# Turning B, C and decay rows on VectorE in 32x32 blocks of 4-byte words, in place of PE transposes

## The chip, the cores and the metric

The kernel runs on one core of a Trainium2 chip. A core has TensorE (PE in the profile; PEld is its weight load), VectorE (DVE), ScalarE (ACT), GpSimd (POOL) and SyncE (SP). They run their own instruction streams and wait for each other through semaphores. Transfers between HBM and the on-chip memory SBUF are issued here by SP and ACT. Matmul results land in PSUM. The metric is device time in microseconds (us) of one execution.

## What is computed

A chunked state-space scan over 4 sequences x 8 heads x 768 steps (head dimension 32, state 16), then a two-layer feed-forward net on its output, seen as 3072 tokens x 256.

```python
for c in range(nc):                       # chunks along a sequence
    cum = np.cumsum(log_a[:, :, sl], axis=-1)
    L = np.exp(cum[:, :, :, None] - cum[:, :, None, :]) * causal
    M = np.einsum('bhin,bhjn->bhij', Cc, Bc) * L
    y[:, :, sl] = M @ xc + (Cc @ state) * exp(cum)
    state = decay_full * state + sum_j decay_from_j * outer(Bc, xc)
g = gelu_tanh(y_as_tokens @ w_in)         # w_in 256 x 2048
out = g @ w_out                           # w_out 2048 x 256
```

The kernel uses chunks of 128 steps (24 in all, six to a sequence). It needs, for each chunk, B scaled by the suffix products of the decays a, with the 8 x 16 (head, state) pairs on partitions (`bh`), C divided by the same products, also with (head, state) on partitions and split by the parity of the head (`ce`), and B with steps on partitions (`bn`).

## The kernel before

**Units.** The chunks go through in units: chunk 0, chunk 1, and then eleven pairs. For a unit PE computes the chunk scores (`f_G`, L408, into the PSUM tile `gb`), DVE masks them (`f_M`, L418), PE makes the state update (`f_D`, L429) and y (`f_Y`, L451 and L460, into `yb`), ACT copies y out as bf16 (`f_yev`, L469, into `xm`). Then come the first matmul of the net (`f_s1`, L506), the activation (`f_gelu`, L514), the second matmul (`f_s2`, L523), the copy out of PSUM (`f_oev`, L530 or L532) and the store (`f_store`, L536).

**Preparing a sequence.** `f_clip` and `f_R` (L272, L276) form decay products in rows, one partition for each (half, sequence, head). `f_RT` (L293) and `f_RT0` (L282) turn them on PE by matmuls with an identity, `f_recip` (L305) inverts them, `f_pp`/`f_pend` (L316, L321) spread the whole-chunk products. `f_mul` (L349) scales B and C of a whole sequence, with steps on partitions; `f_T` (L358) turns six 128x128 blocks of each on PE into PSUM; `f_E` (L365, recorded at the copy helper's lines L256 or L260) copies them to SBUF; `f_F` (L373) makes `ce`; `f_N` (L379) turns `bh` back to steps on partitions and `f_bn` copies that out. The first chunk has its own short path (`f_mul0`, `f_T0`, `f_ce0`, `f_bh0`).

**Loads.** `load_bc` (L154) brings B or C of a sequence in one transfer of 384 KB; `load_bc0` (L148) brings the first chunk alone in 64 KB; `load_x` (L240) brings 128 KB a chunk; `load_wi` (L248) and `load_wo` (L252) bring the weights in quarters of 512 KB. `f_wi` (L264, recorded at L258 or L260) casts a quarter of w_in to bf16 and reorders its columns as it casts, so that `f_s1` loads 128 adjacent columns; `f_wo` casts w_out as it lies.

**Order.** `run_order` places the nodes made by `add` on the engines, by due times (`prio`), given durations and the number of buffers in each pool. The engines then run in exactly that order. While PE has nothing planned, `idle` fills in matmuls on a tile of zeros (L776).

Of the kernel before, what the change touches and what calls it, by code (L numbers as in the profile page):

```python
# [91 lines left out]

@with_exitstack
def kernel(
# [9 lines left out]
):  # L104
    nc = tc.nc
# [3 lines left out]
    Q = 128  # L109
    CPB = S // Q  # L110
    R6 = CPB
    NCH = batch * CPB
    HC = CPB // 2
    HS = S // 2
    d_ff = moe_w_in.shape[1]
    d_model = moe_w_in.shape[0]
    n_tokens = batch * S
    NF = d_ff // 128
    UNITS = [[0], [1]] + [[c, c + 1] for c in range(2, NCH, 2)]
# [3 lines left out]
    ld = ctx.enter_context(tc.tile_pool(name="ld", bufs=batch))  # L123
    wfp = ctx.enter_context(tc.tile_pool(name="wfp", bufs=6))
    ldx = ctx.enter_context(tc.tile_pool(name="ldx", bufs=NU))
    xpool = ctx.enter_context(tc.tile_pool(name="xpool", bufs=6))
    work = ctx.enter_context(tc.tile_pool(name="work", bufs=2))
    msb = ctx.enter_context(tc.tile_pool(name="msb", bufs=4))
    st = ctx.enter_context(tc.tile_pool(name="st", bufs=4))
    GT_BUFS = 6  # L130
    gpool = ctx.enter_context(tc.tile_pool(name="gpool", bufs=GT_BUFS))
    opool = ctx.enter_context(tc.tile_pool(name="opool", bufs=6))
# [5 lines left out]


    a_t = const.tile([64, HS], FP32, name="a_t")  # L140
    a_half = [bass.AP(tensor=a.tensor, offset=a.offset + i * HS, ap=[[S, batch * H], [1, HS]])
              for i in range(2)]
    XF, X16 = {}, {}
    U = [dict() for _ in range(batch)]
    bc0 = const.tile([128, 2, H, N], FP32, name="bc0")

    def load_bc0(i, q):
        q.dma_start(out=bc0[:, i], in_=(B, C)[i][0, :, 0:Q, :].rearrange("h p n -> p h n"))  # L148

    def load_bc(b, i):  # L150
        d = U[b]
        if "bc" not in d:
            d["bc"] = ld.tile([128, 2, H, R6 * N], FP32, name="bc_t")
        nc.sync.dma_start(out=d["bc"][:, i],  # L154
                          in_=(B, C)[i][b].rearrange("h (p r) n -> p h (r n)", r=R6))

    nc.sync.dma_start(out=a_t[0:32], in_=a_half[0])
    nc.scalar.dma_start(out=a_t[32:64], in_=a_half[1])
    load_bc0(1, nc.sync)
    load_bc0(0, nc.scalar)  # L160

    wz = const.tile([128, 512], BF16, name="wz")
# [3 lines left out]
    nc.scalar.activation(warm, warm, AF.Gelu_apprx_tanh)  # L166
    ends = const.tile([64, Q], FP32, name="ends")
    nc.vector.memset(ends, 0.0)
    nc.vector.memset(ends[:, Q - 1:Q], 1.0)
    ac = const.tile([64, HS + 1], FP32, name="ac")  # L170
    nc.vector.memset(ac[:, HS:HS + 1], 0.0)
    pe1 = const.tile([64, HC], FP32, name="pe1")
    pe2 = const.tile([64, 2 * batch, HC], FP32, name="pe2")

    idf = const.tile([64, 64], FP32, name="idf")
    nc.gpsimd.memset(idf, 0.0)
    nc.gpsimd.affine_select(out=idf, in_=idf, pattern=[[-1, 64]], compare_op=ALU.not_equal,
                            fill=1.0, base=0, channel_multiplier=1)
    ident = const.tile([128, 128], BF16, name="ident")
    make_identity(nc, ident)  # L180
    bmask = const.tile([128, H * D], BF16, name="bmask")
    nc.gpsimd.memset(bmask, 1.0)
    bm3 = bmask.rearrange("p (h d) -> p h d", h=H)
    nc.gpsimd.affine_select(out=bm3, in_=bm3, pattern=[[-N, H], [0, D]],
                            compare_op=ALU.is_ge, fill=0.0, base=0, channel_multiplier=1)
    nc.gpsimd.affine_select(out=bm3, in_=bm3, pattern=[[N, H], [0, D]],
                            compare_op=ALU.is_ge, fill=0.0, base=N - 1, channel_multiplier=-1)
# [4 lines left out]
    sel8 = const.tile([64, H], FP32, name="sel8")  # L192
    nc.vector.tensor_reduce(out=sel8, in_=idf.rearrange("p (b h) -> p h b", h=H),
                            op=ALU.add, axis=mybir.AxisListType.X)
    selp = const.tile([64, H, N], FP32, name="selp")
    nc.vector.tensor_copy(out=selp, in_=sel8.rearrange("p (h o) -> p h o", o=1)
                          .to_broadcast([64, H, N]))
    m8 = const.tile([64, 2 * batch], FP32, name="m8")
    nc.gpsimd.memset(m8, 1.0)
    nc.gpsimd.affine_select(out=m8, in_=m8, pattern=[[-H, 2 * batch]], compare_op=ALU.is_ge,  # L200
                            fill=0.0, base=0, channel_multiplier=1)
    nc.gpsimd.affine_select(out=m8, in_=m8, pattern=[[H, 2 * batch]], compare_op=ALU.is_ge,
                            fill=0.0, base=H - 1, channel_multiplier=-1)
    par = const.tile([128, 2], FP32, name="par")
# [5 lines left out]
    r_t = const.tile([64, HS], FP32, name="r_t")  # L210

    rt = const.tile([128, R6, batch * H], FP32, name="rt")
    pt = const.tile([128, R6, batch * H], FP32, name="pt")
    q0 = const.tile([128, H], FP32, name="q0")
    bc0s = const.tile([128, 2, H, N], BF16, name="bc0s")
    ce0 = const.tile([128, 2, Q], BF16, name="ce0")
    bh0 = const.tile([128, Q], BF16, name="bh0")
    pend = const.tile([128, NCH], FP32, name="pend")
    WF = {}
    w_in_sb = const.tile([128, 2, d_ff], BF16, name="w_in_sb")  # L220
    w_out_sb = const.tile([128, NF, d_model], BF16, name="w_out_sb")
    xm = const.tile([128, 2, n_tokens], BF16, name="xm")


    gb = ps1.tile([128, 4, 512], FP32, name="gb")
    yb = ps1.tile([128, 512], FP32, name="yb")
    y4 = yb.rearrange("p (c w t) -> p c w t", c=2, w=2)
    rp0 = yb[:, 0:H]
    T6 = [gb[:, 2 * i, 0:S // 2].bitcast(BF16) for i in range(2)]
    T6_0 = [yb[:, 0:S // 2].bitcast(BF16), T6[1]]  # L230

    T0, DT, MT, RP = {}, {}, {}, {}
    state = {}
    gts, ops, hps, outs = {}, {}, {}, {}

    def load_x(u):
        b, c = divmod(UNITS[u][0], CPB)
        XF[u] = ldx.tile([128, 2, H, D], FP32, name="x_t")
        for k in range(len(UNITS[u])):
            nc.sync.dma_start(out=XF[u][:, k], in_=x[b, :, (c + k) * Q:(c + k + 1) * Q, :]  # L240
                              .rearrange("h p d -> p h d"))

    wi = moe_w_in.rearrange("(k d) f -> d k f", d=128)
    wo = moe_w_out.rearrange("(q p k) m -> q p k m", p=128, k=4)

    def load_wi(q):
        WF[("i", q)] = wfp.tile([128, 2, 512], FP32, name="wf")
        nc.sync.dma_start(out=WF[("i", q)], in_=wi[:, :, q * 512:(q + 1) * 512])  # L248

    def load_wo(q):  # L250
        WF[("o", q)] = wfp.tile([128, 4, d_model], FP32, name="wf")
        nc.sync.dma_start(out=WF[("o", q)], in_=wo[q])  # L252
# [9 lines left out]
    def f_wi(q, k0, k1, eng):  # L262
        for k in range(k0, k1):
            copy(eng, w_in_sb[:, k, q * 512:(q + 1) * 512].rearrange("d (k p) -> d k p", k=4),  # L264
                 WF[("i", q)][:, k].rearrange("d (p k) -> d k p", k=4))

    def f_wo(q, eng):
        copy(eng, w_out_sb[:, 4 * q:4 * q + 4], WF[("o", q)])


    def f_clip(i0, i1):
        nc.vector.tensor_scalar(out=ac[:, i0:i1], in0=a_t[:, i0:i1], scalar1=1e-6, scalar2=1.0,  # L272
                                op0=ALU.max, op1=ALU.min)

    def f_R(k):
        nc.vector.tensor_tensor_scan(out=r_t[:, k * Q:(k + 1) * Q][:, ::-1],  # L276
                                     data0=ac[:, k * Q + 1:(k + 1) * Q + 1][:, ::-1],
                                     data1=ends[:, ::-1], initial=1.0,
                                     op0=ALU.mult, op1=ALU.max)

    def f_RT0():
        nc.tensor.matmul(out=rp0, lhsT=r_t[0:32, 0:Q], rhs=idf[0:32, 0:H], start=True, stop=True,  # L282
                         skip_group_check=True)

    def f_RT(r0, r1):
        if r0 == 0:
            RP[1] = psh.tile([128, 512], FP32, name="hp")[:, 0:R6 * batch * H] \
                .rearrange("p (r j) -> p r j", r=R6)
        r6 = r_t.rearrange("q (p r) -> q r p", r=R6)
        for r in range(r0, r1):  # L290
            for i in range(2):
                rs = slice(32 * i, 32 * i + 32)
                nc.tensor.matmul(out=RP[1][64 * i:64 * i + 64, r], lhsT=r6[rs, r],  # L293
                                 rhs=idf[rs, rs], start=True, stop=True,
                                 tile_position=(32 * i, 64 * i), skip_group_check=True)
# [517 lines left out]
```

## Time and profile before

| | us |
|---|---|
| Median of 3 runs (124.72 to 125.45) | 125.07 |
| Span of the profiled execution, first to last instruction | 122.8 |
| PE busy in it | 114.6 (93%) |
| DVE / ACT / POOL busy | 68.3 / 74.9 / 23.0 |
| Mean of one activation (L514), 96 of them | 0.596 |
| Mean of one mask (L418, 128x1024), 23 of them | 1.217 |
| Mean of one scaling of B or C (L349, 128x768) | 0.95 |
| Mean of one w_in cast on POOL (L258, 128x512), 6 of them | 1.193 |
| Median, issue to landing: a quarter of w_in / a chunk of x / a store | 6.9 / 4.5 / 1.7 |

PE's busy time counts its pipelined matmuls and the fill on zeros, so a busy PE is not a PE at its useful peak. The row PEclk of the profile gives the clock that PE was granted, in tenths.

### The profile page before, as it was taken

How to read it: one execution, taken by the hardware profiler on the slowest of the kernel's cores; microseconds unless marked ns; L12 is line 12 of the kernel's file. 1: busy time of each engine (PE TensorE's matmuls, PEld its weight loads, DVE VectorE, ACT ScalarE, POOL GpSimd, SP SyncE). 2: the span in 40 equal slices, each digit the busy share in tenths (PEclk: the TensorE clock that was granted, in tenths of full speed). 3: DMA queues.
4: the chain of work that ended last, by engine and by line, in shares of the span. 5: the costliest groups of instructions: out<-in, count | busy, mean ns of one | idle time of the engine just before them, and what ended most of it. 6: DMA issues, size and time to landing. Idle time of an engine off the chain costs nothing.

```text
span 122.8 us, 3507 instructions
## 1 busy us (share of the span) xinstructions
PE 114.6 (93%) x1506; PEld 96.2 (78%) x1506; DVE 68.3 (56%) x116; ACT 74.9 (61%) x145; POOL 23.0 (19%) x38
## 2 busy tenths in 40 slices
PE   5899978989799999999999999999999999999970
PEld 5687747778678798787879889787878888888860
DVE  3897999968849888184979672475663000000110
ACT  4025536674676677656686777865768766786310
POOL 7206967750320160122000000000000000000000
PEclk9975699999999999999999999999999999999999
DMA  3999959989799899851101101101110111100121
GB/s 52 242 266 265 328 112 370 320 191 200 128 229 221 127 235 216 145 134 48 43 0 48 43 0 48 43 0 48 43 43 5 45 43 45 45 21 22 43 90 43
DMA packets 40591, 14.09 MB, mean 115 GB/s; under 512 B 35904, under 2 KB 39040, under 8 KB 40576
## 3 DMA queue, kind: packets, MB, share of 16 engines
q1 hardware_dynamic: 39488, 13.75, 46.4%
q8 instruction: 12, 0.20, 0.7%
q10 hardware_dynamic: 1088, 0.11, 0.7%
q14 instruction: 3, 0.02, 0.1%
HBM read 10.72 MB, written 3.15 MB: 113 GB/s over the span
## 4 chain that ended last, share of the span: by engine, by line
PE 70%; SPq 18%; DMA 5%; DVE 3%; issue 1%; DVEq 0%
PE o_ps L523 29%; PE hp L506 29%; SPq L240 7%; DMA bc_t<-in_B_dram 5%; SPq L252 5%; SPq L154 4%; PE yb L523 3%; SPq L248 3%; PE gb L408 2%; PE yb L451 2%; PE yb L460 2%; PE gb L358 2%; DVE ch L260 2%; PE gb L379 1%; DVE bc L349 1%
## 5 line engine op out<-in xcount | busy, mean ns | idle before, releaser
L514 ACT ACTIVATE gT<-hp 128x512 bf16<-128x512 f32 x96 | 53.6, 596 | 24.4 <-PE hp L506 24.2
L506 PE MATMUL hp<-xm,w_in_sb 128*128 128x256 bf16 (+1 forms) x416 | 53.7, 267 | 0.9 <-POOL w_in_sb L258 0.4
L523 PE MATMUL o_ps<-w_out_sb,gT 128*128 128x256 bf16 x352 | 47.3, 273 | 0.0
L506 PEld LDWEIGHTS <-w_in_sb 128*128 128x128 bf16 x416 | 37.6, 99 | 7.7 <-issue 2.0
L523 PEld LDWEIGHTS <-gT 128*128 128x128 bf16 x384 | 37.1, 98 | 4.8 <-issue 0.4
L418 DVE TENSOR_TENSOR m<-gb,tri 128x1024 bf16<-128x1024 f32 (+1 forms) x25 | 29.1, 1173 | 1.9 <-PE gb L408 1.8
L532 DVE COPY o_sb<-o_ps 128x256 f32<-128x256 f32 x2 | 0.8, 424 | 25.6 <-PE o_ps L523 25.6
L258 POOL CAST x<-x_t 128x512 bf16<-128x512 f32 (+1 forms) x12 | 8.5, 710 | 25.0 <-DMA x_t<-in_x_dram 20.1
L479 DVE SCALAR_TENSOR_TENSOR s_new<-s_new,pend,hp 128x64 f32<-128x64 f32 x16 | 4.5, 279 | 11.5 <-PE hp L429 11.2
L776 PE MATMUL o_ps<-wz 128*128 128x128 bf16 x77 | 8.9, 267 | 1.3 <-DVE warm L165 1.3
L530 ACT ACTIVATE o_sb<-o_ps 128x256 f32<-128x256 f32 x20 | 7.7, 385 | 3.8 <-PE o_ps L523 2.1
L486 DVE SCALAR_TENSOR_TENSOR sp_new<-s_new,pend,bmask 128x256 bf16<-128x256 f32 x20 | 10.0, 506 | 0.0
L469 ACT ACTIVATE xm<-yb 128x512 bf16<-128x512 f32 (+1 forms) x13 | 7.3, 564 | 4.3 <-PE yb L460 2.1
L258 POOL CAST w_in_sb<-wf 128x512 bf16<-128x512 f32 x6 | 7.0, 1193 | 7.0 <-DMA wf<-in_moe_w_in_dram 7.0
L776 PEld LDWEIGHTS <-wz 128*128 128x128 bf16 x77 | 6.5, 122 | 1.8 <-DVE warm L165 1.2
L460 PE MATMUL yb<-m,x 128*32 128x128 bf16 x192 | 6.3, 223 | 0.6 <-DVE m L418 0.6
L373 DVE TENSOR_SCALAR ce<-ch,par 128x768 bf16<-128x768 bf16 (+2 forms) x10 | 5.9, 634 | 0.8 <-ACT ch L256 0.8
L451 PE MATMUL yb<-ce,sp_new 128*32 128x128 bf16 x160 | 5.3, 221 | 0.0
L408 PE MATMUL gb<-ce,bh 32*128 32x256 bf16 x96 | 5.1, 278 | 0.0
L460 PEld LDWEIGHTS <-x 128*32 128x32 bf16 x192 | 3.8, 97 | 1.5 <-issue 1.5
L358 PEld LDWEIGHTS <-bc 128*128 128x128 bf16 x48 | 3.8, 110 | 1.3 <-issue 1.1
L258 POOL CAST w_out_sb<-wf 128x1024 bf16<-128x1024 f32 x4 | 4.4, 1112 | 1.5 <-DMA wf<-in_moe_w_out_dram 1.5
(72 smaller groups left out, 61.6 us busy)
## 6 DMA issues: line engine op xcount, KB each, us to landing
x_t<-in_x_dram SPq DMA_DIRECT2D x24, 128.0 KB, 4.5
out_dram<-o_sb SPq DMA_DIRECT2D x24, 128.0 KB, 1.7
wf<-in_moe_w_in_dram SPq DMA_DIRECT2D x4, 512.0 KB, 6.9
wf<-in_moe_w_out_dram SPq DMA_DIRECT2D x4, 512.0 KB, 6.0
bc_t<-in_C_dram SPq DMA_DIRECT2D x4, 384.0 KB, 4.4
bc_t<-in_B_dram SPq DMA_DIRECT2D x4, 384.0 KB, 5.4
bc<-in_B_dram ACTq DMA_DIRECT2D x1, 64.0 KB, 4.2
bc<-in_C_dram SPq DMA_DIRECT2D x1, 64.0 KB, 2.8
```

Of the source, the lines that this page charges most:

```text
L240: nc.sync.dma_start(out=XF[u][:, k], in_=x[b, :, (c + k) * Q:(c + k + 1) * Q, :] .rearrange("h p d -> p h d"))
L258: nc.gpsimd.tensor_copy(out=o, in_=i)
L408: nc.tensor.matmul(out=gb[:, g, 256 * k:256 * k + 256], lhsT=bh_of(gc)[32 * g:32 * g + 32], rhs=ce_of(gc)[32 * g:32 * g + 32], start=True, ...
L418: nc.vector.tensor_tensor(out=MT[gc][:, g0:g1], in0=gb[:, g0:g1, 256 * k:256 * k + 256] .rearrange("p g (e t) -> p g e t", e=2), in1=tri_b ...
L451: nc.tensor.matmul(out=y4[32 * j:32 * j + 32, k, w], lhsT=sp[:, 32 * h:32 * h + 32], rhs=ce_of(gc)[:, h % 2], start=first(j), stop=False, ...
L460: nc.tensor.matmul(out=y4[32 * j:32 * j + 32, k, w], lhsT=X16[u][:, k, 32 * h:32 * h + 32], rhs=m[:, h // 2, h % 2, :], start=first(j), st ...
L486: nc.vector.scalar_tensor_tensor(out=sp_new.rearrange("p (g d) -> p g d", g=4), in0=state[("s", gc)].rearrange("p (o d) -> p o d", o=1).to ...
L506: nc.tensor.matmul(out=hp[:, j * nt:(j + 1) * nt], lhsT=w_in_sb[:, kc, fi * 128:(fi + 1) * 128], rhs=xm[:, kc, t0:t0 + nt], start=(kc == 0 ...
L514: nc.scalar.activation(gts[u][:, i * per:(i + 1) * per, 0:nt], hps.pop((u, i)).rearrange("p (j t) -> p j t", j=per), AF.Gelu_apprx_tanh)
L523: nc.tensor.matmul(out=ops[gc], lhsT=gts[u][:, fi, tt * Q:(tt + 1) * Q], rhs=w_out_sb[:, fi, :], start=(fi == 0), stop=(fi == NF - 1), ski ...
L530: nc.scalar.activation(o_sb, ops.pop(gc), AF.Copy)
L776: nc.tensor.matmul(out=zb[:, 0:128], lhsT=wz[:, 0:128], rhs=wz[:, 0:128], start=True, stop=True)
```

## The change

- **Transposes.** `f_T` now runs on DVE: pairs of neighbouring steps of bf16 make 4-byte words, and a word tile is turned in 32x32 blocks, from SBUF to SBUF. The loads put four (head pairs) x 32 partitions with 4 steps each side by side, so that blocks of 32 are enough. `f_E`, the PE transposes of B and C, the PE turns of the decays and the first chunk's own path are gone. `f_N`/`f_bn` stay on PE and ACT.
- **Decays.** Each sequence has its own `f_clip`, `f_scan`, `f_rT` (a DVE turn), `f_qT` (reciprocals, in groups of chunks) and `f_pend` (four small DVE instructions).
- **Groups.** The first sequence is prepared in groups of 1, 1, 2 and 2 chunks, the others in two groups of 3. `f_mul` is two instructions for each group, since it interleaves the steps.
- **`f_F`** masks with a bitwise AND on 4-byte integers.
- **Loads.** B and C of the first sequence come in 24 transfers of 32 KB (4 issued by ACT, 20 by SP), those of the others in 8 transfers of 96 KB each. x of the later sequences comes in one transfer of 768 KB for each sequence.
- **w_in** is cast as it lies, half of quarters 0 to 2 by ACT, the rest by POOL; `f_s1` picks every fourth column as it loads weights.
- **Units.** Chunks 0 to 3 are units of one, then pairs. `gT` has 5 buffers (6 before).
- **Last chunk.** Its second matmul is done in two halves of 128 columns, each copied out (DVE, ACT) and stored by itself.
- **Order.** A table `PRIO` gives each node a due time of its own.

```diff
+PRIO = {
+    'SP0': -401.905, "load_bc0(0, 1, 1, 'ACT')": 389.204, "load_bc0(1, 0, 1, 'ACT')": 586.494,
...
+    UNITS = [[0], [1], [2], [3]] + [[c, c + 1] for c in range(4, NCH, 2)]
...
+    def load_bc(b, i, g, q):
+        t = get("bc", b, [128, 2, 2 * CPB * R, N], FP32)
+        src = (B, C)[i]
+        QS[q].dma_start(out=t[32 * g:32 * g + 32, i].rearrange("p (k r) n -> p k (r n)", r=R),
+                    in_=bass.AP(tensor=src.tensor, offset=src.offset + (b * H + 2 * g) * S * N,
+                                ap=[[R * N, 32], [Q * N, 2 * CPB], [1, R * N]]))
+
+    def load_bc0(c, i, e, q):
...
+        QS[q].dma_start(out=t[:, i, k:k + R].rearrange("p r n -> p (r n)"),
+                    in_=bass.AP(tensor=src.tensor, offset=src.offset + e * S * N + c * Q * N,
+                                ap=[[2 * S * N, 4], [R * N, 32], [1, R * N]]))
...
+    def load_xs(b):
+        t = get("xs", b, [128, H * CPB, D], FP32)
+        nc.sync.dma_start(out=t, in_=bass.AP(tensor=x.tensor, offset=x.offset + b * H * S * D,
+                                             ap=[[D, Q], [Q * D, H * CPB], [1, D]]))
...
+    w_in5 = w_in_sb.rearrange("d k (q p j) -> d k q j p", q=4, j=4)
...
-            copy(eng, w_in_sb[:, k, q * 512:(q + 1) * 512].rearrange("d (k p) -> d k p", k=4),
-                 WF[("i", q)][:, k].rearrange("d (p k) -> d k p", k=4))
+    def f_wi(q, k, eng):
+        copy(eng, w_in_sb[:, k, q * 512:(q + 1) * 512], T[("wf", ("i", q))][:, k])
...
+    def f_rT(i):
+        nc.vector.transpose(out=rT[i].rearrange("p k r -> p r k"),
+                            in_=rr[i].rearrange("q (p r) -> q r p", r=R))
+
+    def f_qT(b, c0, c1):
+        o, v = (t[b][:, K0[b]:K0[b] + 2 * CPB] for t in (qT, rT))
+        if c1 - c0 < CPB:
+            o, v = (t.rearrange("p (e c) r -> p e (c r)", e=2)[:, :, R * c0:R * c1] for t in (o, v))
+        nc.vector.reciprocal(o, v)
...
+        for k in range(2):
+            nc.vector.tensor_tensor(
+                out=t[:, ss, :, :, k].rearrange("p s e n -> p e s n"), in0=v[:, :, ss, k],
+                in1=w[:, :, ss, k:k + 1].to_broadcast([128, 2, 2 * (c1 - c0), N]), op=ALU.mult)
+
+    def f_T(b, i, c0, c1):
+        t = get(("bT", "cT")[i], b, [128, S], BF16)
+        nc.vector.transpose(
+            out=t[:, c0 * Q:c1 * Q].bitcast(FP32).rearrange("q (c p s) -> q c s p", p=32, s=2),
+            in_=T[("bc16", (b, i))][:, 2 * c0:2 * c1].rearrange("p s e n k -> p (s e n k)").bitcast(FP32)
+            .rearrange("p (c s j) -> p c s j", s=2, j=32))
+
+    def f_F(b, c0, c1):
...
+            nc.vector.tensor_scalar(out=t[:, e, c0 * Q:c1 * Q].bitcast(I32),
+                                    in0=T[("cT", b)][:, c0 * Q:c1 * Q].bitcast(I32),
+                                    scalar1=pari[:, e:e + 1], scalar2=None, op0=ALU.bitwise_and)
...
-                                 lhsT=w_in_sb[:, kc, fi * 128:(fi + 1) * 128],
+                                 lhsT=w_in5[:, kc, fi // 4, fi % 4],
...
+    def f_s2h(h):
+        u, tt = UNIT_OF[NCH - 1]
+        o = gb[:, 2 * h, 0:128]
+        for f in range(NF):
+            nc.tensor.matmul(out=o, lhsT=T[("gT", u)][:, f, tt * Q:tt * Q + Q],
+                             rhs=w_out_sb[:, f, 128 * h:128 * h + 128], start=(f == 0),
+                             stop=(f == NF - 1), skip_group_check=True)
...
+    GROUPS = [[(0, 1), (1, 2), (2, 4), (4, 6)]] + [[(0, 3), (3, 6)]] * (batch - 1)
...
+    for n in nodes:
+        n.prio = PRIO.get(n.name, n.prio)
```

More of the change, by code (lines that the diff above doesn't have):

```diff
@@ L165 @@
     nc.vector.memset(warm, 0.0)
[L166 to L178, printed above, removed]
+    nc.vector.memset(zeros, 0.0)
+    for i in range(batch):
+        nc.vector.memset(rr[i][:, Q - 1:Q], 1.0)
     ident = const.tile([128, 128], BF16, name="ident")
     make_identity(nc, ident)
[L181 to L187, printed above, removed]
     tri = const.tile([128, Q], BF16, name="tri")
@@ L273, in f_clip, with f_warm, f_scan @@
+    def f_warm():
+        nc.scalar.activation(warm, warm, AF.Gelu_apprx_tanh)
+    def f_clip(i):
+        nc.vector.tensor_scalar(out=ac[i], in0=at[i], scalar1=1e-6, scalar2=1.0,
                                 op0=ALU.max, op1=ALU.min)
[L275 to L278, printed above, removed]
+    def f_scan(i):
+        nc.vector.tensor_tensor_scan(out=rr[i][:, 0:Q - 1][:, ::-1], data0=ac[i][:, 1:Q][:, ::-1],
+                                     data1=zeros[:, 0:Q - 1], initial=1.0,
@@ L355, in f_T @@
-    def f_T(b, i):
-        bc = U[b]["bc16"].rearrange("p i r h n -> p i r (h n)")
-        for r in range(R6):
-            nc.tensor.transpose(out=(T6 if b else T6_0)[i][:, r * 128:(r + 1) * 128], in_=bc[:, i, r], identity=ident)
-    def f_E(b, i, eng, p0=0, p1=128):
-        d = U[b]
-        nm = ("bh", "ch")[i]
-        if nm not in d:
-            d[nm] = work.tile([128, S], BF16, name=nm)
-        copy(eng, d[nm].rearrange("q (p r) -> q p r", r=R6)[:, p0:p1],
-             (T6 if b else T6_0)[i].rearrange("q (r p) -> q p r", r=R6)[:, p0:p1])
@@ new lines, in f_N, with f_bn @@
+    def f_N(b, c0, c1, where):
+        t = (gb[:, 1] if where == "gram" else psh.tile([128, 512], FP32, name="hp"))
+        T[("N", b, c0)] = t = t[:, 0:S // 2].bitcast(BF16)
+        for c in range(c0, c1):
+            nc.tensor.transpose(out=t[:, c * Q:(c + 1) * Q],
+                                in_=T[("bT", b)][:, c * Q:(c + 1) * Q], identity=ident)
+    def f_bn(b, c0, c1, eng):
+        t = get("bn", b, [128, CPB, 128], BF16)
+        copy(eng, t[:, c0:c1].rearrange("p c n -> p (c n)"), T[("N", b, c0)][:, c0 * Q:c1 * Q])
@@ L624, with load_bc0_n @@
-    mul_b = add("DVE", 0.97, f_mul, 0, 0, deps=[bl[(0, 0)], RTa, mul_c], prio=-20)
-    rtc = add("ACT", 0.33, f_rtc, deps=[RTa, mul_b], prio=-60)
-    RTa.takes("hp", rtc)
-    rc2 = add("DVE", 1.35, f_recip, 1, batch, deps=[rtc], prio=45)
-    RT0.prio = -99
-    ppn = add("PE", 0.4, f_pp, deps=[pen], prio=-28)
-    pendn = add("ACT", 0.2, f_pend, deps=[ppn], prio=-29)
-    ppn.takes("hp", pendn)
+                win_l[q] = load(1.58, load_wi, q)
+    b0l = {}
+    def load_bc0_n(*cs, act=True):
+        for c in cs:
+            for i in (0, 1):
+                b0l[(c, i)] = [load(0.16, load_bc0, c, i, e, q="ACT" if act and e else "SP", iss=0.45)
+                               for e in (0, 1)]
@@ new lines @@
+    load_bc0_n(0)
+    wrm = add("ACT", 1.3, f_warm, prio=-150)
+    xl[0] = load(0.87, load_x, 0)
+    load_w_n(0)
+    load_bc0_n(1)
+    load_w_n(1)
+    xl[1] = load(0.87, load_x, 1)
+    load_w_n(2, 3)
+    load_bc0_n(2, act=False)
+    xl[2] = load(0.87, load_x, 2)
+    load_bc0_n(3, act=False)
+    load_w_n(0, o=True)
+    xl[3] = load(0.87, load_x, 3)
+    load_w_n(1, 2, 3, o=True)
+    load_bc0_n(4, 5, act=False)
+    xl[4] = load(0.87, load_x, 4)
+    xl[5] = load(0.87, load_x, 5)
+    for b in range(1, batch):
+        an[b] = load(0.2, load_a, b)
+        load_bc_n(b, 0)
+        load_bc_n(b, 1)
+        n = load(5.2, load_xs, b)
+        for c in range(CPB):
+            xl[CPB * b + c] = n
@@ new lines @@
+    for q in range(4):
+        es = (("POOL", 0.6), ("ACT", 0.67)) if q < 3 else (("POOL", 0.6), ("POOL", 0.6))
+        win[q] = [add(e, t, f_wi, q, k, e, deps=[win_l[q]], prio=-60 + q) for k, (e, t) in enumerate(es)]
+        won[q] = add("POOL", 1.1, f_wo, q, "POOL", deps=[won_l[q]], prio=20 + q)
+        win_l[q].issue.takes("wf", *win[q])
+        won_l[q].issue.takes("wf", won[q])
+    rn, pen = {}, {}
+    for b in range(batch):
+        p0 = -100 if b == 0 else 10.0 * CPB * b - 31
+        cl = add("DVE", 0.25, f_clip, b, deps=[an[b]], prio=p0)
+        sc = add("DVE", 0.43, f_scan, b, deps=[cl], prio=p0 + 0.1)
+        rn[b] = add("DVE", 0.41, f_rT, b, deps=[sc], prio=p0 + 0.2)
+        pen[b] = add("DVE", 0.55, f_pend, b, deps=[sc], prio=-74 if b == 0 else p0 + 0.3)
@@ L673, with bnp @@
+    def bnp(b, c0, c1, deps, q, where):
+        nn = add("PE", 0.1 + 0.06 * (c1 - c0), f_N, b, c0, c1, where, deps=deps, prio=q)
+        bb = add("ACT", 0.18 + 0.08 * (c1 - c0), f_bn, b, c0, c1, "ACT", deps=[nn], prio=-65 if b == 0 else -45)
+        nn.takes(where, bb)
+        for c in range(c0, c1):
+            bnn[CPB * b + c] = bb
     for u, cs in enumerate(UNITS):
@@ L778, in idle @@
         return fill
-    pools = {"hp": 2, "o": 1, "gram": 1, "yb": 1, "wf": 6, "ob": 6}
-    for t, fn in run_order(nodes, pools, idle=idle, wait=("DVE", "POOL")):
+    pools = {"hp": 2, "o": 1, "gram": 1, "yb": 1, "wf": BUFS["wf"], "ob": BUFS["ob"]}
+    order = run_order(nodes, pools, idle=idle, wait=("DVE", "POOL"))
+    for t, fn in order:
         fn()
```

515 lines of the change are left out of this document (192 added, 323 removed), and 128 rows, old and new, of the table PRIO.

## The prediction

> **What bounds the kernel now.** I read the slices first, then the chain of waits, then PE's windows, then the timeline of the start. In the slices of the whole span (about 3.1 us each), PE is full from the tenth on; the granted clock and the load on the DMA engines say what the first third looks like:
>
> ```profile
> span 122.8 us, 3507 instructions
> PE   5899978989799999999999999999999999999970
> PEclk9975699999999999999999999999999999999999
> DMA  3999959989799899851101101101110111100121
> ```
>
> The clock is low from about 6 to 15 us, and DMA is near full, but for one slice, until 50 us. The chain that ended last, in order of time, has this around 30 us, and from 31.7 on almost nothing but PE:
>
> ```profile
> 24.08 5.77 DMA bc_t<-in_B_dram
> 29.87 0.96 DVE bc L349
> 30.82 0.88 DVE ch L260
> 31.74 0.49 PE gb L358 x6
> ...
> 34.32 0.87 PE hp L506 x8
> ...
> 66.57 0.33 PE gb L358 x6
> ...
> 119.10 0.42 DVE o_sb L532
> ```
>
> So 256 columns of the net cost 0.87/8 = 0.109 us, a transpose 0.33/6 = 0.055. Before 31.7 the end is set by transfers and the casts behind them. The windows of L506 alone (busy us and count of PE, of PEld, clock, DMA share, GB/s) show how little of the net is done early: by 24 us, 64 matmuls of half width.
>
> ```profile
> 0.00:24.00 24.00, 6.01 (x64) 4.25 (x64) 0.86 0.91 246
> 24.00:32.00 8.00, 3.88 (x28) 2.65 (x28) 1.00 1.01 186
> 32.00:119.10 87.10, 43.81 (x324) 30.69 (x324) 1.00 0.33 75
> ```
>
> The timeline of the start tells why:
>
> ```profile
> 10.04 2.13 POOL L258 CAST w_in_sb<-wf 128x512 bf16<-128x512 f32 x2 [5.85 <-DMA wf<-in_moe_w_in_dram]
> 12.51 2.21 DVE L373 TENSOR_SCALAR ce<-ch,par 128x384 bf16<-128x384 bf16 x2
> 17.02 2.06 DVE L260 CAST w_in_sb<-wf 128x512 bf16<-128x512 f32 x2
> 18.65 0.10 PEld L506 LDWEIGHTS <-w_in_sb 128*128 128x128 bf16 x1 [0.57 <-POOL w_in_sb L258]
> 20.86 3.17 SPq L154 DMA_DIRECT2D bc_t<-in_C_dram  x1
> ```
>
> The last quarter of w_in is cast at 19.1; the second sequence's C is issued from 20.9 and its B lands at 29.8.
>
> **A ledger for PE.** Counted at warm prices (0.109 us a net matmul of 256 columns, 0.055 a transpose, 0.33/8 a score matmul, 0.113/8 a matmul of y), all useful PE work of before is 98.5 us; 90.2 of it is left at 24.0, and PE ends at 119.0: it loses 4.8 us after 24. Of the work left, 36 transposes (three sequences x 2 x 6) are removed by the change.
>
> **The change, part by part.**
>
> *Transposes out of PE's stream.* 36 x 0.0547 = 2.0 us of a stream that sets the end: -2.0. The first sequence's twelve and the decay turns lie in the start, priced below.
>
> *DVE in their place.* Removed for each later sequence: two scalings at 0.955, two copies at 0.955, two `ce` at 0.475, 4.8 us. Added: eight half scalings of 192 words at 0.36 (between 0.291 for 128 and 0.955 for 768), 2.9; two reciprocals of 48 at 0.457, 0.9; `f_clip`, `f_scan`, `f_pend` at 0.19 + 0.41 + 4 x 0.17, 1.3; four masks of `f_F`, 0.25 to 0.36 each, 1.2; and the block turns, which the trace does not show. Bounds for a turn of 192 words: from the scaling row, a word a step, 0.36; from the slowest per-element DVE row but the reciprocal, the scan (0.413 for 128), 0.62. I take 0.36, since a turn is a copy without a recurrence: four make 1.4, with the decay turn 1.7. Sum 8.0, +3.2 a sequence. With masks, states and state products (6 x 1.217 + 5 x 0.27 + 5 x 0.506 = 11.2) DVE has 19.2 us for each 23.7 us of PE: hidden in the stream, by 4.5 us.
>
> *The start.* From the built order and rows of before: an issue of a small load costs SP 0.41 to 0.47, a small load lands 2.0 to 2.8 after issue, and in the built order each load waits for the one eight loads earlier to land. In before the halves of megabytes land every 1.7 to 2.6 us (9.99, 12.39, then with 128 KB between 14.46 and 17.09). Now the first quarter of w_in is SP's second issue (1.2) instead of its fifth (4.55), and only 64 KB + 4 x 32 KB go beside it: landing about 5. The second is SP's tenth; ahead of it x of chunk 0 waits for the first quarter, so issue about 6, landing 9.3. The third is the eighteenth and waits for the second: issue 9.6, landing 13. The fourth is the twenty-fifth, behind six small loads one of which waits for w_out's first quarter: issue 13, landing 16. A cast as it lies costs POOL 1.112/2 = 0.56 (the w_out row, twice the width) instead of 1.193, so the last is done near 17.2 instead of 19.1. On PE: y of chunk 0 needs two small B loads issued by ACT after its table load (3.2, landed 5.5) and then scaling, turn, mask; DVE's chain (four dependent `f_pend` steps at 0.27 apart, reciprocals at 0.2 to 0.26 among them) gives scores at 8.5 and y at 10.4, copied out behind ACT's cast of quarter two at about 11: no earlier than the 10.45 of before. From there six groups of s1 (2.6 us) are free to run before the last quarter instead of PE waiting on casts. Following PE's order: s1 of unit 1's last quarter near 17.7, y of chunk 2 at 18.2 (mask 17.8), w_out's quarters cast at 19.6, 21.1 and 23.4. By 24.0 this is 12 groups of s1 (5.2), four of s2 (1.7), six chunks of scores, five units' transposes and y: 9.0 us of work that both kernels do, where before has 6.3. So -2.7.
>
> *Its discount.* DVE has about 20 us of instructions between 3.4 and 27 in this plan, and rows of before show it slowed there: two `ce` of 384 columns took 2.21 us beside POOL's casts, when 768 take 0.475 later. If two of the new masks meet that, DVE is 1 to 1.7 us late, and y of chunks 2 to 5 with it. I add +1.0 (ends 0 and +2.3).
>
> *The second sequence.* PE's 0.62 us idle before 31.74 goes away if B and C come by then: after the last x of the first sequence (about 25) 768 KB at the 1.35 and 1.65 that its two halves took land near 28.5, scaled and turned by 30.5, when PE wants them: -0.6 (bounds 0, -0.9). x of that sequence is now one transfer behind them; six chunks at the 0.5 to 0.9 between x landings make 34, and its first cast (0.735) ends at 35, where PE's order wants it near 35: +0.7 (bounds 0, +1.5). Everything on SP queues behind it, the first stores too, but six output buffers cover those.
>
> *The end.* Two halves of 16 x 0.055 instead of 16 x 0.109, and a copy of 128 columns (0.28, as the 128x128 row of ACT) instead of 0.42: -0.1. What follows the copy, 0.33 + 1.4 to landing and 1.5 to the end, stays.
>
> Small loads are where a rule of the Trainium skill speaks against the change: "DMA: Bandwidth & Descriptors", section "Rules for kernel authors", says that transfers under 64 KB pay mostly overhead and should be joined. By it the 24 loads of 32 KB would cost little less than 24 of 64 KB; what that gives is the second rival. The rule for the strided weight load is in "SBUF — State Buffer", "Door 1": it puts the free stride at 8 bf16 or 4 fp32 elements, of which the new load uses 4. By that the third rival has no price, and the old cast's penalty (1.193 against 0.56, a stride of four fp32) is more than the page would give it, so I keep the rival.
>
> *Sum* against the profiled execution: 122.8 - 2.0 - 2.7 + 1.0 - 0.6 + 0.7 - 0.1 = 119.1 of span. The median shown is 2.3 above the span (125.07 against 122.8): 121.4.
>
> **The rivals.**
>
> *DVE too slow in the start and in each hand-over (0.14).* For: the 2.21 us row, and DVE at eight to nine tenths in slices 11 to 18 already. Against: 4.5 us of slack a sequence by the rows. With turns at the scan's price, 4 x 0.26 = 1.0 more a sequence, and masks at 1.1 beside POOL, the discount becomes its upper end and the wait for x 1.5: 121.4 + 1.3 + 0.8 + 0.4 = 123.9.
>
> *Small loads hold up the weights (0.14).* For: 25 issues on SP ahead of w_in's last quarter (eleven in before, with bigger loads). If each of the last 17 waits as long as loads of before took in a backlog (5.5 us for eight), it is issued at 4.4 + 17 x 0.69 = 16.1, lands at 21.6, is cast at 22.8, 3.7 after before. Then the start's -2.7 is lost and 3.7 is added less 1.3 for the six groups done meanwhile: 125.4, both sides of no change. Against: those landings were of 128 to 512 KB.
>
> *The strided weight load (0.10, the slower side).* `f_s1` now picks every fourth column. The trace has no strided bf16 weight load; POOL's strided cast cost twice the plain one. Weight loads of 128 adjacent columns keep pace with matmuls of 128 columns (0.055). Doubled to 0.11, the 256-column matmuls barely notice (320 x 0.003 = 1.0), but units 0 to 3 have 128 of 128 columns: +7.2, half of it inside the start's waits at best. 126.0 to 129.6; I put 128. It decides once a load passes 0.055 + 3.7/128 = 0.084 us. Below nothing there is no bound: no load gets faster.
>
> *The gain is given back (0.06).* Only the removed transposes count, and an order by 400 single due times leaves PE waiting elsewhere: about 124.8.
>
> **How the numbers follow.** Forecast 0.56 at 121.4; by its own terms 118.0 (no discount, clock not lowered at 6 to 15) to 124.2. A difference under 0.5% (124.45 to 125.70) counts as none, about what a measurement here can tell. Faster: 0.56 + 0.11 of the DVE rival + 0.02 = 0.69. Same: 0.03 + 0.05 + 0.02 = 0.10. Slower: 0.10 + 0.07 + 0.04 = 0.21. The range reaches to the middle of the strided rival: 118.0 to 127.0, leaving out about 0.08 below and 0.10 above.
>
> **What would show it.** No 128x128 transposes of B and C in PE's rows, and 24 left for `bn`. The last cast of w_in near 17 (right) or past 20 (small loads). Weight loads of w_in still at 99 ns mean, and eight half-width matmuls in 0.45 us (else the strided rival). In the chain, no DMA piece of 5 us at 24 to 30, PE from some 28 us on. Turns of 192 words at 0.36 or 0.62. PE's end at 115.4 instead of 119.0. I am wrong if PE waits on DVE's scalings or masks in the stream, or if PE's ledger at 24 us is under 8 us.

## The result, and the profile after

| | before | after |
|---|---|---|
| Median (4 runs each) | 124.89 us (124.51 to 125.45) | 134.3 us (133.22 to 134.6) |
| Span of the profiled execution | 122.8 | 132.3 |
| PE busy | 114.6 | 113.0 |

The ratio is 1.072, 95% interval [1.066, 1.078]: 9.4 us slower, where 3.7 faster was forecast and 127.0 was the top of the range. Some executions come out over 1.5% longer than the fastest of their kernel; ratios and intervals here leave them out, medians do not. In the slices of after (3.3 us each), PE has two holes, not one:

```profile
span 132.3 us, 3556 instructions
...
PE   6406994299899997786799999999999999999990
...
PEclk9955589657999999999999999999999999999999
DMA  1547665996999678999941111011001110011121
```

One hole is the start, with the DMA engines mostly at four to seven tenths where before had nine. The other is in slices 16 to 20, from 50 to 67 us, where before was full. The windows of all engines (busy us and count of PE, PEld, DVE, ACT, POOL, then clock, DMA share, GB/s) put numbers to both; first after, then before:

```profile
0.00:8.00 8.00, 3.79 (x42) 3.62 (x42) 3.05 (x20) 2.12 (x3) 2.90 (x12) 0.95 0.34 98
8.00:16.00 8.00, 5.00 (x55) 3.46 (x56) 5.65 (x24) 1.83 (x5) 1.02 (x2) 0.50 0.72 189
16.00:24.00 8.00, 5.05 (x75) 4.45 (x73) 3.09 (x11) 4.16 (x8) 1.66 (x2) 0.91 0.61 170
...
50.00:70.00 20.00, 16.08 (x211) 13.15 (x210) 15.19 (x41) 11.95 (x22) 3.56 (x6) 1.00 1.06 159
```

```profile
0.00:8.00 8.00, 6.18 (x70) 5.29 (x70) 5.36 (x23) 1.76 (x3) 3.11 (x16) 0.98 0.83 166
8.00:16.00 8.00, 7.77 (x85) 5.80 (x84) 7.05 (x11) 4.51 (x11) 5.70 (x6) 0.59 1.04 285
16.00:24.00 8.00, 6.90 (x140) 5.46 (x140) 7.72 (x12) 3.98 (x8) 5.73 (x6) 1.00 0.86 287
...
50.00:70.00 20.00, 20.00 (x295) 16.91 (x294) 14.51 (x22) 13.55 (x27) 1.84 (x3) 1.00 0.27 64
```

The ledger of the prediction, with the same prices, splits the 9.9 us by which PE ends later (128.9 against 119.0). Work left at 24.0: 90.8 against 90.2. Time lost after 24.0: 14.1 against 4.8, namely 4.6 against 2.0 from 24 to 32, 2.1 against 0.9 to 50, 5.9 against 0.7 to 70, 1.6 against 1.2 beyond.

*The start.* The DMA view of 4.5 to 9.0 us, in 40 slices of 0.11 us, shows the small loads of B and C nearly alone on the queues from 5.2 us on, when most of the first w_in quarter is through (its last part lands at 7.2), until x is issued at 7.5:

```profile
DMA  7776425112422222233223333333333333336899
```

Two to three tenths of 16 engines are busy, while SP waits 2.5 us for a load of B before it issues x. At 34 to 37 us, with loads of the later sequences (the same 256-byte packets, 32 partitions and 96 KB each), the share is 0.95. A difference in the code is the outermost dimension: 4 in `load_bc0`, 32 in `load_bc`. What the small loads hold up stands in the chain that ended last (start, us) and in the timeline of the last w_in quarter:

```profile
1.96 5.49 DMA bc<-in_B_dram
```

```profile
20.61 0.48 SPq L375 DMA_DIRECT2D wf<-in_moe_w_in_dram  x1
24.97 1.17 POOL L385 CAST w_in_sb<-wf 128x512 bf16<-128x512 f32 x2 [4.31 <-DMA wf<-in_moe_w_in_dram]
```

A load of 32 KB takes 5.5 us, and the last cast of w_in ends at 26.1.

*50 to 67 us.* The timeline of PE in after (start, us, instruction, idle time before it):

```profile
57.17 0.63 PE L583 MATMUL hp<-xm,w_in_sb 128*128 128x256 bf16 x4
57.63 0.60 PE L601 MATMUL o_ps<-w_out_sb,gT 128*128 128x256 bf16 x4
58.48 0.60 PE L583 MATMUL hp<-xm,w_in_sb 128*128 128x256 bf16 x4 [0.25 <-ACT gT L592]
58.91 0.60 PE L601 MATMUL o_ps<-w_out_sb,gT 128*128 128x256 bf16 x4
59.76 0.60 PE L583 MATMUL hp<-xm,w_in_sb 128*128 128x256 bf16 x4 [0.25 <-ACT gT L592]
```

A group of s1 starts every 1.28 us, each behind the gelu of the group right before it, though `hp` has two buffers. The other was last used by a state update, read by DVE at 57.24. The trace has 13 groups that start between 50 and 66.5 us, and each of them starts after the gelu of the one before has ended, as if the pool gave every group the buffer of its predecessor. In the list of waits of before there is none of s1 on a gelu; in after they make 4.9 us (total, times, longest):

```profile
PE hp L583 <- ACT gT L592: 4.9, 9, 1.1
```

### The profile page after: what moved, and what is told of

The parts are those of the page before. It is cut to its first block, busy times and chain, and to the rows that moved or that the text cites. A ratio compares the mean times of both kernels' runs of the same rounds, so it can differ in the third digit from the quotient of the medians.

```text
span 132.3 us, 3556 instructions
## 1 busy us (share of the span) xinstructions
PE 113.0 (85%) x1475; PEld 97.5 (74%) x1475; DVE 72.3 (55%) x196; ACT 76.1 (58%) x146; POOL 16.9 (13%) x34
## 4 chain that ended last, share of the span: by engine, by line
PE 67%; SPq 13%; DMA 8%; ACT 4%; DVE 3%; issue 2%; ACTq 1%; DVEq 0%
PE hp L583 30%; PE o_ps L601 25%; DMA bc<-in_B_dram 8%; SPq L311 7%; ACT gT L592 4%; PE yb L601 3%; PE gb L492 2%; SPq L375 2%; PE yb L533 2%; PE yb L542 2%; SPq L379 2%; SPq L317 2%; PE gb L616 1%; ACTq L311 1%; PE gb L459 1%
## 5 line engine op out<-in xcount | busy, mean ns | idle before, releaser
L583 PEld LDWEIGHTS <-w_in_sb 128*128 128x128 bf16 x448 | 44.4, 117 | 10.2 <-issue 7.1
L383 ACT ACTIVATE ob<-o_ps 128x256 f32<-128x256 f32 x20 | 7.7, 385 | 4.4 <-PE o_ps L601 2.4
L567 DVE SCALAR_TENSOR_TENSOR sp<-st,pend,bmask 128x256 bf16<-128x256 f32 x20 | 9.7, 486 | 0.0
L385 POOL CAST x<-xs 128x512 bf16<-128x512 f32 x9 | 5.5, 641 | 29.7 <-DMA xs<-in_x_dram 28.0
L561 DVE SCALAR_TENSOR_TENSOR st<-st,pend,hp 128x64 f32<-128x64 f32 x16 | 4.2, 264 | 8.7 <-PE hp L512 8.5
L436 DVE TENSOR_TENSOR bc<-bc,qT 128x192 bf16<-128x192 f32 (+2 forms) x20 | 6.6, 378 | 3.6 <-DMA bc<-in_C_dram 3.4
L436 DVE TENSOR_TENSOR bc<-bc,rT 128x192 bf16<-128x192 f32 (+2 forms) x20 | 5.3, 326 | 5.9 <-DMA bc<-in_B_dram 5.9
L492 PE MATMUL gb<-ce,bT 32*128 32x256 bf16 x96 | 5.6, 292 | 2.1 <-DVE bT L443 2.1
L451 DVE TENSOR_SCALAR ce<-cT,pari 128x192 int32<-128x192 int32 (+2 forms) x20 | 4.9, 293 | 1.7 <-PE gb L492 1.6
L533 PE MATMUL yb<-ce,sp 128*32 128x128 bf16 x160 | 5.5, 226 | 0.2 <-DVE sp L567 0.2
```

The source lines that it names most:

```text
L383: nc.scalar.activation(o, i, AF.Copy)
L436: nc.vector.tensor_tensor(out=t[:, ss, :, :, k].rearrange("p s e n -> p e s n"), in0=v[:, :, ss, k], in1=w[:, :, ss, k:k + 1].to_broadcast ...
L492: nc.tensor.matmul(out=gb[:, g, 256 * k:256 * k + 256], lhsT=bT_of(gc)[32 * g:32 * g + 32], rhs=ce_of(gc)[32 * g:32 * g + 32], start=True, ...
L533: nc.tensor.matmul(out=y4[32 * j:32 * j + 32, k, w], lhsT=sp[:, 32 * h:32 * h + 32], rhs=ce_of(gc)[:, h % 2], start=first(j), stop=False, ...
L567: nc.vector.scalar_tensor_tensor(out=t.rearrange("p (g d) -> p g d", g=4), in0=T[("s", gc)].rearrange("p (o d) -> p o d", o=1).to_broadcas ...
L583: nc.tensor.matmul(out=hp[:, j * nt:(j + 1) * nt], lhsT=w_in5[:, kc, fi // 4, fi % 4], rhs=xm[:, kc, t0:t0 + nt], start=(kc == 0), stop=(k ...
```

## The experiments

Times are medians; the kernel before, run beside each batch, was between 124.49 and 125.25.

**1. The same loads on 16 engines.** The scaled tile keeps its layout; each load of 32 KB now fills 32 partitions with chunks j and j+3 of two heads. DVE, ACT, PE and POOL keep their order; since chunks come in pairs, 16 loads stand in front where 8 stood. ACT issues 8 of the 24, where it issued 4.

```diff
-    in_=bass.AP(tensor=src.tensor, offset=src.offset + e * S * N + c * Q * N,
-                ap=[[2 * S * N, 4], [R * N, 32], [1, R * N]])
+    in_=bass.AP(tensor=src.tensor, offset=src.offset + 2 * g * S * N + j * Q * N,
+                ap=[[R * N, 32], [3 * Q * N, 4], [1, R * N]])
```

> The 24 loads of the first sequence's B and C keep their number, their 32 KB and their 256-byte packets, but each now fills 32 partitions (outermost dimension 32) in place of four groups of 32 (outermost dimension 4); 16 of them, not 8, stand ahead of x and of most weights, and the order on the other engines is the one before. Theory A (an outermost dimension of 4 keeps a load on about 4 of the 16 DMA engines, and that starves the weights): the DMA share of 0 to 24 us rises from 0.56 to over 0.75, the last w_in quarter is cast by 22 us (26.1 before), the PE has done at least 6 us of work by 24 us (3.9 before), and the time falls by 2 to 4 us, to 130 to 132. Theory B (24 loads of 32 KB cost their issue, 0.53 us each, and the wait for one of eight places, whatever engines carry them): nothing gained, the weights come later by up to 4 us, time 134 to 138.

Measured: 130.21 us, 4.1 less. Its windows:

```profile
0.00:8.00 8.00, 4.66 (x42) 4.40 (x42) 3.79 (x24) 1.76 (x3) 2.91 (x12) 1.00 0.48 127
8.00:16.00 8.00, 5.20 (x54) 3.51 (x55) 5.52 (x20) 2.23 (x6) 1.02 (x2) 0.57 0.95 222
16.00:24.00 8.00, 6.41 (x84) 5.22 (x83) 5.38 (x16) 4.54 (x9) 3.08 (x5) 0.79 0.77 216
24.00:32.00 8.00, 6.97 (x125) 5.58 (x124) 7.25 (x17) 4.79 (x10) 4.38 (x7) 1.00 0.91 228
```

The time agrees with A (the gain a little past its bound) and excludes B, but three of A's signs failed: the share of 0 to 24 us is 0.73, not over 0.75, the last w_in cast ends at 23.76, not by 22, and 4.3 us of useful work is done by 24, not 6. The gain came just after: 2.1 us lost from 24 to 32 against 4.6.

That four issues went from SP to ACT can't be told apart by the time. The landing events in the traces show the engines without it: in after each of these loads has one event at its issue and then four landings, in experiment 1 the same 32 KB has 16, as every load of before has. The load of 5.5 us above lands in four parts, from 6.05 to 7.44 us; the first one in experiment 1, issued at 0.8, is whole at 2.63.

**2. Two buffers in turn.**

```diff
-        hp = psh.tile([128, 512], FP32, name="hp")
+        hp = next_hp()        # hp0, hp1, hp0, ... in the plan's order
```

> The two PSUM buffers of the first layer's groups are fixed and taken in turn, in the order in which the plan gives them; nothing else is changed. Theory H (from 50 to 67 us only one of the two buffers is in use, so that each group of eight matmuls waits for the gelu of the group right ahead of it): the groups' period there falls from 1.29 us to about 0.9, the PE's wait for the gelu (4.9 us in all) to under 1.5 us, and the time falls by 4 to 6 us, to 128 to 130. Rival X (the late x of the second sequence and the state updates on VectorE set this stretch, and the groups only fill it): the time stays within 1 us of 134.3.

Measured: 129.74 us, 4.6 less. H holds. The same stretch of PE's timeline:

```profile
57.09 0.60 PE L588 MATMUL hp<-xm,w_in_sb 128*128 128x256 bf16 x4
57.53 0.60 PE L606 MATMUL o_ps<-w_out_sb,gT 128*128 128x256 bf16 x4
57.97 0.60 PE L588 MATMUL hp<-xm,w_in_sb 128*128 128x256 bf16 x4
58.40 0.60 PE L606 MATMUL o_ps<-w_out_sb,gT 128*128 128x256 bf16 x4
```

The groups start 0.87 us apart, and s1 waits 1.5 us for the gelu in all. PE is busy 19.34 of the 20 us from 50 to 70.

**3. Both.** 

> Both edits. If A and H are right and act at different dates, the gains add: 6 to 10 us, to 124 to 128. If the start's loss is made up later anyhow (the state chain of the later sequences sets the end), the two together give no more than the larger of them.

Measured: 125.65 us (ratio to before 1.007 [1.002, 1.011]). 4.1 + 4.6 = 8.7, and both together give 8.65: two separate losses that together are nearly all of the 9.4.

**4. Another order of the first loads** (on 3).

```diff
+    at_ = "load_bc0(1, 1, 1, 'ACT')"
+    for nm in ('load_x(0,)', 'load_wi(1,)', 'load_wi(0,)', 'load_x(1,)', ...):
+        move(nm, at_)
+        at_ = nm
```

> Both edits of the run before (16 engines, two buffers in turn, 125.65 us) and another order of the first loads, with the same loads: the first w_in quarter moves from ahead of B and C to behind the first x, w_in's other quarters stand ahead of w_out's first, and the casts that would now be waited for too early move behind their neighbours. Theory C (what the start still lacks is order: the first w_in quarter holds up B and C until 5.9 us, w_out's first quarter holds up w_in's last two): y(0) about 2 us earlier, last w_in quarter cast by 19 us (23.6 in the run before), time 122 to 124. Rival D (the DMA engines are full from 8 to 16 us, share 0.95, so bytes decide and order moves nothing): within 0.5 us of 125.6.

Measured: 125.45 us: D. The matmuls of y(0) ran at 10.25, where the forecast had them, but PE then stood 4.4 us before the second state update for an x that landed at 14.6; the last w_in cast ended at 22.4.

**5. That order with the loads on four engines.** Edit 4 on 2. 

> The same new order and the two buffers in turn, but the 24 loads of B and C in the changed kernel's form (outermost dimension 4); to be read against the run with the two buffers alone (129.7 us) and against the new order with the 16-engine loads. Theory A: the order can't help while these loads hold about 4 engines each; the time stays 3 us or more above the 16-engine form in the same order, at 126 to 130. If order was the cause all along: within 1 us of the 16-engine form.

Measured: 130.08 us, at the upper end of A, against 129.74 (old order) and 125.45 (16 engines). Order does nothing on either side; the engines make 4.6 us.

**6. The w_in cast through the stride again** (on 4).

```diff
-        copy(eng, w_in_sb[:, k, q * 512:(q + 1) * 512], T[("wf", ("i", q))][:, k])
+        copy(eng, w_in_sb[:, k, q * 512:(q + 1) * 512].rearrange("d (j p) -> d j p", j=4),
+             T[("wf", ("i", q))][:, k].rearrange("d (p j) -> d j p", j=4))
```

> The new order with both edits, and one part of the change undone: w_in is cast through the four-way stride again (1.193 us a half on the cast engine before, 0.61 us as it lies), the weight load is contiguous again. The forecast's reading: the casts are 0.58 us longer each, eight of them, four in a row on POOL at the start, so the last quarters come 1 to 2 us later and the time rises by 0.5 to 1.5 us. Rival (the strided weight load of the new form costs as much in the stream as the casts save): within 0.5 us, or lower, and the matmuls of the first layer closer together.

Measured: 126.12 us, +0.67, with overlapping intervals (1.0063 to 1.0198 and 1.0025 to 1.0109 of before): the sign is that of the forecast, but neither it nor the size is clear of the noise.

**7. A second order** (on 3).

```diff
+    move("f_wi(1, 1, 'ACT')", "f_yev(0,)")
+    move("f_D(1,)", "f_s1(0, 1)")
+    move("f_S(1, 0)", "f_D(1,)")
```

> Both edits and a second order of the first loads: the second x stands ahead of w_in's second quarter, the first y copy stands ahead of ScalarE's two w_in casts, and the state matmuls of the second chunk stand behind the first group of the first layer, so that they no longer hold it up (in the order before, y(0) was done at 10.5 us and its copy-out ended at 14.93, behind two casts; the state matmuls waited 4.4 us for the second x). Theory C: first group at 13 us in place of 16.1, useful PE work done by 24 us 5.5 to 6.5 in place of 4.3, time 123 to 124.3. Rival D (the DMA engines are full from 8 us on, so the next weight quarter is what is waited for instead): within 0.5 us of 125.45.

In this kernel and the next, the second group of s1 of chunk 0 is written over the first before its gelu has read it: no instruction is left out, but one wait is (its matmuls start at 15.14 us, that gelu at 16.22). Measured: 125.86 us. D again: PE now waited 3.5 us for w_in casts in place of x. The queue ahead of the weights is what is left: the first w_in quarter is issued at 6.15, behind 18 other loads.

**8. Three times the transposes that are left** (on 7).

```diff
-        for c in range(c0, c1):
+        for c in [c for c in range(c0, c1) for _ in range(3)]:
```

> The kernel of the run beside it, with each of the 24 PE transposes that are left (B turned back for the state matmuls) done three times over into the same place, 48 more transposes in all; the result is the same. It prices the term of the forecast that took 36 transposes out of the stream at 0.055 us each. If the PE's stream is the bound where they lie: 48 x 0.055 = 2.6 us more, 2.0 to 3.2. If they lie in time in which the PE waits: under 0.6 us more.

Measured: 126.52 us, +0.66, between the two expectations. In the trace six transposes in a row take 0.34 us and eighteen 1.01, so the price holds; but the start differed by more than that between the two executions. Repeated as 10.

**9. Eight loads in place of 24** (on 2, order near 7, with the second state update behind both groups of chunk 0).

```diff
     def load_bc0(c, i, e, q):
+        if c < 2:
+            load_bc(0, *FRONT[q].pop(0), q)     # i, g: 8 loads of 96 KB
```

> The two buffers in turn, and the first sequence's B and C loaded whole, by 8 loads of 96 KB with outermost dimension 32 (four on each queue) in place of 24 of 32 KB; then x, w_in, x, w_in and so on as in the run before, with the state matmuls of the second chunk behind both groups of the first. Until now 16 to 24 small loads stood ahead of the weights, each issued every 0.45 us, and the DMA share from 0 to 8 us was 0.44. Theory E (with the engines all in use, it is the issue of small loads that leaves the DMA idle early): share of 0 to 8 us over 0.6, first w_in quarter issued at 4 us in place of 6.15, w_in quarters cast 1.5 to 2.5 us sooner (by 10.5, 13, 16.5, 20), time 123 to 124.5 against 125.86. Rival F (all six chunks have to land before the first turn, so that y(0) comes later by as much): first turn after 8.5 us, time 125.5 or more.

Measured: 122.65 us, ratio to before 0.983 [0.979, 0.987]: faster than both kernels. Its windows:

```profile
0.00:8.00 8.00, 4.66 (x42) 4.40 (x42) 3.29 (x22) 1.49 (x2) 2.29 (x11) 1.00 0.89 138
8.00:16.00 8.00, 5.66 (x69) 4.13 (x69) 5.80 (x21) 3.08 (x8) 1.86 (x4) 1.00 1.03 307
16.00:24.00 8.00, 5.98 (x115) 4.75 (x112) 7.82 (x21) 5.11 (x11) 5.34 (x8) 1.00 0.92 279
```

The DMA engines are now full from the start and move 307 GB/s from 8 to 16 us where after had 189. F's date came true (first turn at 9.56, after 7.2 in experiment 7), and cost nothing that counted: the last w_in cast ends at 18.6. E holds in its share (0.89) and in its last date; the first w_in quarter was issued at 5.65, not at 4, and the time is a little under its range.

**10. Experiment 8 on this kernel.** 

> The kernel of the run beside it with each of its 24 transposes done three times over into the same place (48 more, 36 of them in the second to fourth sequence, in the stream); same result. In the same test on the kernel before, six transposes in a row took 0.34 us and eighteen 1.01, so 0.056 us each. If all that the stream holds after 30 us is on the path: 36 x 0.056 = 2.0 us more, and up to 0.7 of the first sequence's twelve. If waits elsewhere swallow it: under 0.8.

Measured: 125.03 us, +2.4 (ratio 1.002 [0.999, 1.005] against 0.983 [0.979, 0.987]), between the 2.0 of the stream and the 2.7 of all 48. What stands in PE's stream after the start is paid in full.

**11. Eight loads in the changed kernel's own order.** Edits 2 and 9 without any move. 

> As the 8-load kernel (122.65 us), but every other load, cast and matmul in the changed kernel's own order: the first w_in quarter ahead of B and C, w_out's first quarter ahead of w_in's last two, the state matmuls of the second chunk ahead of the first group. It tells how much of that kernel's gain over the kernel with 24 16-engine loads (125.65) is the number of loads and how much is order. If number and issue decide: 122.5 to 123.5. If order decides once the issue is out of the way: 124.5 to 126.

Measured: 122.63 us (ratio 0.981 [0.977, 0.985]). All of the gain over experiment 3, 3.0 us, comes with the eight loads; order gives none of it. The edit changes more than their number: all six chunks come first, and SP has four loads of B and C ahead of x where it had eight; no run tells these apart. So after with two small edits, eight loads and two buffers in turn, beats before by 1.9%.

**12. Strided cast on 9.** Edit 6. 

> The 8-load kernel in its own order with the w_in cast through the four-way stride again (1.193 us a half on the cast engine before, 0.61 as it lies) and a contiguous weight load. In the 24-load kernel this cost 0.67 us (126.12 against 125.45), hardly more than the runs' spread. Here w_in's quarters are cast as soon as they land, and POOL casts its last three halves in a row: 0.8 to 1.8 us more (123.4 to 124.4) if the casts are on the path; under 0.5 if they are hidden; less than 122.4 if the strided weight load slows the stream.

Measured: 126.83 us, but with runs from 123.83 to 127.77: no size can be given. What its trace shows is under the hardware below.

## Why the prediction was wrong

**The step that failed first: the landing of the small loads, and with it every date in the start.** The prediction let a small load land 2.0 to 2.8 us after its issue, and the first quarter of w_in at 5, because "only 64 KB + 4 x 32 KB go beside it"; the next three came at 9.3, 13 and 16, by the pace at which megabytes landed in before. Every small load was so taken as bytes at the full rate of 16 engines. A load with outermost dimension 4 has four of them: a load of B took 5.5 us, the scores of chunk 0 ran at 12.0 (forecast 8.5) and its y at 14.6 (10.4). The first quarter of w_in was nearly right (15 of its 16 parts landed by 5.9, the last at 7.2), but the second was issued at 10.1 (forecast 6) and the last cast ended at 26.1 (17.2). By 24 us PE had done 3.9 us of useful work, not 9.0: the term of -2.7 came out at +2.4, and 2.6 more was lost from 24 to 32. The prediction's own sign of being wrong, a ledger under 8 us at 24, had come true. The rule was there to be read: the Trainium skill, "DMA: Bandwidth & Descriptors", section "Rules for kernel authors", says that the outermost dimension bounds the engines that a transfer uses. The trace agrees: four landings a load, 0.2 to 0.3 of 16 engines, and 4.1 us back with dimension 32. I used that section only for its line on small transfers, the lesser part here: 3.0 us (experiments 3 and 11).

**The step that was not there: PSUM buffers.** No term covered 50 to 70 us; the sum took the stream as full, as in before. The `hp` pool has two buffers, as the plan assumes, but those that the build hands out are not in turn. That was 4.6 us (experiment 2).

**Rivals.** "Small loads hold up the weights" had the right place and sign and too small a price: issue of the last quarter at 16.1, where it was 20.6, since its pace too came from loads on 16 engines. "The gain is given back" expected that PE would wait elsewhere, as it did from 50 to 67 us, but laid it to the order and saw no loss in it beyond the gain. "DVE too slow" is not what happened: in experiment 9, with the same DVE work, PE is busy all of 32 to 70 us. The strided weight load leaves the pace as it was: in after, eight matmuls of 256 columns still take 0.87 us, and those of 128 columns start 0.056 us apart. One of its signs failed all the same: a weight load of w_in takes 117 ns in the mean (114 in experiment 9), not 99.

**Terms that held.** The transposes: 2.0 us, by 0.056 us each in the trace and by experiment 10. The turn of 192 words on DVE: 0.36 to 0.37 us in the mean, forecast 0.36. DVE's work for a later sequence: 7.9 us by the rows of after, forecast 8.0. The cast as it lies: 0.61 us, forecast 0.56.

**The start's gain was never there.** With the two losses taken out (experiment 3) the kernel runs at 125.65 us, 4.3 above the forecast of 121.4. Experiment 11, at 122.6, is near the forecast only because eight loads take out 3.0 us more, and not by the forecast's sum. Its span is 2.4 below that of before: PE ends 2.0 earlier, at 117.0, as much as the transposes are worth, and the stretch from PE's end to the end of the span is 3.4 us in place of 3.8, where 0.1 was forecast. By 24 us PE has done 5.8 us of useful work, still less than the 6.3 of before. So the -2.7 of the start and its discount of +1.0 came to about nothing there. The -0.6 for the second sequence was not measured by itself.

**x of the second sequence.** Forecast +0.7 with the first cast ending at 35. In after it ended at 45.5 and POOL waited 28.0 us for x in all; in experiment 9, with x loaded the same way, it ended at 37.5 and PE is full beside it. In neither does PE's list of waits have one for that cast: the wait was of an engine with time to spare, and no run shows the 0.7.

**Slips in the working.** The 2.0 to 2.8 us of a small load leave out a row of before: the 64 KB of B that ACT issued took 4.2. In before the first quarter of w_in was SP's sixth issue, not its fifth, and nine issues, not eleven, stood ahead of the last. The 125.4 of the second rival comes out only without the discount of 1.0; with it, it is 126.5.

## What to carry to other kernels

Before costing a load by its bytes, look at its outermost dimension and then at the DMA share while it runs alone: here 0.2 to 0.3 of the 16 engines stood for four. Many loads that are each cheap can leave the DMA engines idle early (a share of 0.47 from 0 to 8 us with 24 loads, 0.81 with eight, in the same order); a few large pieces can pay even if the first consumer starts later. When a plan counts on two buffers, check in the built program which one each user waits for.

## What the runs showed that was not expected

A load with outermost dimension 4 takes longer to issue, too: 0.53 to 0.58 us on SP where the queue does not wait, against 0.43 to 0.45 for the same 32 KB with 32. The loads of a in after, also with 4, take 0.55.

Some DVE instructions that start beside a POOL cast end just after it, and others are not held. In experiment 12 the timeline has, with the casts through the stride:

```profile
16.29 2.24 POOL L388 CAST w_in_sb<-wf 128x512 bf16<-128x512 f32 x2 [0.49 <-DMA wf<-in_moe_w_in_dram]
...
16.68 2.01 DVE L440 TENSOR_TENSOR bc<-bc,qT 128x128 bf16<-128x128 f32 x2
```

Two scalings of C take 2.01 us, and each ends 0.15 us after the cast beside it; in experiment 9, with no cast beside them, those of B, of the same shape, are

```profile
L439 DVE TENSOR_TENSOR bc<-bc,rT 128x128 bf16<-128x128 f32 x2 | 0.5, 298 | 0.0
```

In experiment 9 two instructions of `f_F`, of 128 words, meet the short casts: 17.52 to 18.14 beside a cast until 18.07, 18.07 to 18.70 beside one until 18.62. The Trainium skill, "SBUF — State Buffer", section "SBUF: two separate sides", calls the port of the two an exclusive lock, held for a whole instruction; the trace agrees for these. A cast on POOL that is twice as long can so hold DVE twice as long. But a turn is not held. In after, beside a cast of w_out until 33.59:

```profile
32.55 1.04 POOL L385 CAST w_out_sb<-wf 128x1024 bf16<-128x1024 f32 x1 [1.61 <-DMA wf<-in_moe_w_out_dram]
32.58 0.21 DVE L421 STREAM_TRANSPOSE pv<-pv 128x32 f32<-128x32 f32 x1
32.83 0.78 DVE L423 TENSOR_SCALAR pv<-pv,par 128x6 f32<-128x6 f32 x1
```

The turn takes its usual 0.21 us. The step of `f_pend` behind it, 0.23 us with no cast beside it, ends with the cast.

The granted clock halved in the start of most executions and not in others of the same kernel, without a time to show for it: in experiment 3 the run at a mean clock of 0.995 took 125.94 us, one at 0.955 took 125.02. PE has little useful work there.
